# A 256-token first chunk, beta through K=1 matmuls, weights on ScalarE's queue, and key sums on GpSimd, in a fused attention and MLP kernel

## The chip, the cores and the metric

The kernel runs on one core of one Trainium2 chip. The metric is the device time of one execution in microseconds (us). I quote the median of a kernel's runs. A ratio between two kernels is the mean time of one kernel's fast runs over the mean of the other's fast runs of the same rounds, so it is not quite the ratio of the medians that I quote. A run is called slow when it is over 1.5% above the fastest run of the same kernel; ratios use fast runs alone. A profile is one execution: its span (130.2 us for the kernel before) is about 2 us shorter than the measured time.

The engines are named as in the profile: PE is TensorE (matmuls), DVE is VectorE, ACT is ScalarE, POOL is GpSimd, SP is SyncE, which here only issues DMA. This kernel fixes by hand the order in which each engine gets its instructions, and in the traces below an engine that waits for one instruction doesn't go on to the next: in x1_start_loop PE stood 4.58 us at one group of matmuls while the `moeout` products behind it had had their input for 4.1 us. That will matter.

## The reference, cut to what matters

```python
def phi(x):                       # 64 features from two 8-wide sketches
    a = einsum('rd,bhsd->bhsr', S1, x); b = einsum('rd,bhsd->bhsr', S2, x)
    return outer(a, b).reshape(..., 64)
q_p, k_p = phi(q), phi(k)         # q, k, v: (4, 4, 1088, 32) f32
kv  = einsum('bhsf,bhsd->bhfd', k_p, v)
z   = sum(k_p, axis=2)
num = einsum('bhsf,bhfd->bhsd', q_p, kv)
den = einsum('bhsf,bhf->bhs', q_p, z) + 1e-06
x   = (num / den), heads side by side          # (4352, 128)
h   = x @ w_in                                 # (4352, 2048)
out = (h / (1 + exp(-beta * h))) @ w_out       # (4352, 128)
```

There are four batches of 1088 tokens. The attention of a batch must be complete over its keys before any of its tokens can enter the MLP. The MLP is the larger part of the work.

## The kernel before

**The MLP in waves.** Since h·sigmoid(beta·h) is Silu(beta·h)/beta, the kernel folds beta into the weights: `winp = w_in * beta` and `woutp = w_out / beta`. What is left is one Silu per tile. A *wave* is two matmuls of 512 columns into a tile `wave` in PSUM (the memory that takes PE's products here), one Silu of 128x1024 on ScalarE into `g`, and two matmuls into `moeout`. A chunk of 512 tokens is eight waves; the whole MLP is 68 waves. The start time of each Silu is therefore a good clock of progress, and I use it throughout.

**The attention in groups.** Between waves stand small groups: `kps` (sketches of the keys), `kab` (their transposes), `kp` (the outer product), `kvz` (kv and z on PE), `kvd` (their copy out of PSUM by ScalarE), `zb` and `nd` (z and kv turned for the next products), `aps`/`bps` and `qp` (the same for the queries), `ndps`, `dps` (denominator), `dT`, `rc`, `rb` (its inverse, spread out), `nps` (numerator) and `xT`, the MLP's input.

```python
    tok_chk = [(o, min(TCH, NTOK - o)) for o in range(0, NTOK, TCH)]   # TCH = 512
    q_chk = [(0, 9), (9, TP - 9)]                 # 576 and 512 tokens of each batch
    # ... all big loads in one queue, in this order:
    k_t[0] = load_rows(k, 0, "k", halves)
    q_t[0] = load_rows(q, 0, "q", halves)
    v_t[0] = load_v(0)
    for c in range(0, DFF, DFF // 2):             # the weights stand behind q, k, v of batch 0
        nc.sync.dma_start(out=w_in_sb[:, cs], in_=moe_w_in[:, cs])
        nc.sync.dma_start(out=beta_bc[:, cs], in_=...)        # beta broadcast to 128 partitions
        nc.sync.dma_start(out=w_out_sb[:, js, :], in_=...)
    # ... [cut]
    def slot(group, waves):                       # a group of attention, then `waves` waves
        if group is not None:
            group()
        for _ in range(waves):
            if moe["ci"] < len(tok_chk) and sum(tok_chk[moe["ci"]]) > moe["ready"]:
                break                             # this chunk's tokens are not there yet
            # ... w2 of an older wave, then w1 of the next
```

The start, and the loop over batches 1 to 3:

```python
    kps(0); ...                                   # batch 0, first 576 tokens
    keep_warm(2); ndt(0); keep_warm(3)            # matmuls without use, in PE's idle time
    invert = den(0, 0); divide = num(0, 0); invert(); divide()
    turn_q(0, 1)
    keep_warm(9)
    slot(None, 1)                                 # the first wave
    # ... [cut: batch 0's second chunk, 512 tokens, one wave between groups]
    for b in range(1, B):
        if b == 1:
            for h in range(H): outer(b, h)        # kp, on VectorE
        turn_q(b, 1)
        slot(lambda: r_group((b, 1, 0), (b, 0, 0)), 1)
        zs = sum_z(b)                             # four adds on VectorE
        slot(lambda: kv(b, [1, 2, 3, 4], zs), 1 if few else 2)
        # ... [cut]
        turn_k(b + 1)                             # keys of the next batch: in mid-batch
        slot(lambda: kv(b, [5, 6, 7, 8, 0], zs), 1 if few else 2)
        slot(lambda: r_group((b, 1, 1), (b, 0, 1)), 1)
        turn_q(b + 1, 0)
        slot(lambda: kps(b + 1), ...); outer(b + 1, 0)
        # ... [cut: outer(b + 1, 1..3) spread over the next groups]
        slot(lambda: den(b, 0)(), ...)            # one denominator and inverse for each chunk
        slot(num0_den1, 1)
        slot(lambda: num(b, 1)(), 1)
```

## Time and profile before

| | before |
|---|---|
| time, median of 4 runs beside the changed kernel | 132.01 us (131.59 to 132.52) |
| span of the profile, mean granted TensorE clock | 130.2 us, 0.997 |
| first Silu, eighth Silu, 13th, 48th, last | 23.0, 36.8, 46.4, 102.0, 124.0 us |
| Silus that start in 30 to 60 us | 16 |
| busy: PE, VectorE, ScalarE, GpSimd | 113.1, 71.3, 79.8, 11.1 us |

Next, pieces of the chain of waits before the first Silu (start, duration, what):

```profile
1.65 6.04 DMA q<-in_q_dram
...
9.23 1.75 DVE kp L346 x5
...
12.90 4.13 PE kvz L406 x144
...
22.97 1.03 ACT g L267
```

The start takes 23 us: q's load until 7.7, products on VectorE, `kvz` on PE from 12.9 to 17.0, then the short steps to `xT`. Last, the stretch that the change aims at, in the view by stretches. Its columns are the stretch, its length, the busy time and count of PE, PEld, DVE, ACT and POOL, the granted clock, the DMA share and GB/s.

```profile
30.00:60.00 30.00, 27.72 (x356) 10.42 (x354) 27.49 (x48) 19.22 (x22) 0.00 (x0) 1.00 0.47 94
```

VectorE is busy for 27.49 of 30 us.

### The profile page before, as it was taken

How to read it: one execution, taken by the hardware profiler on the slowest of the kernel's cores; microseconds unless marked ns; L12 is line 12 of the kernel's file. 1: busy time of each engine (PE TensorE's matmuls, PEld its weight loads, DVE VectorE, ACT ScalarE, POOL GpSimd, SP SyncE). 2: the span in 40 equal slices, each digit the busy share in tenths (PEclk: the TensorE clock that was granted, in tenths of full speed). 3: DMA queues.
4: the chain of work that ended last, by engine and by line, in shares of the span. 5: the costliest groups of instructions: out<-in, count | busy, mean ns of one | idle time of the engine just before them, and what ended most of it. 6: DMA issues, size and time to landing. Idle time of an engine off the chain costs nothing.

```text
span 130.2 us, 2977 instructions
## 1 busy us (share of the span) xinstructions
PE 113.1 (87%) x1216; PEld 45.9 (35%) x1216; DVE 71.3 (55%) x142; ACT 79.8 (61%) x92; POOL 11.1 (9%) x24
## 2 busy tenths in 40 slices
PE   5787999887889999999997999999999989888830
PEld 2132933222334342342432332443432333334620
DVE  2579119249799988997367579940737400200210
ACT  1303010876358767477777866687776798888930
POOL 3000399700000000000000000000000000000000
PEclk9999999999999999999999999999999999999998
DMA  3999999999992320031000400500032050031232
GB/s 110 304 187 275 358 353 314 208 249 203 235 210 83 56 30 0 5 54 29 5 0 10 71 5 0 81 0 5 0 49 36 0 80 1 0 58 25 35 48 40
DMA packets 24909, 12.42 MB, mean 95 GB/s; under 512 B 18992, under 2 KB 23104, under 8 KB 24896
## 3 DMA queue, kind: packets, MB, share of 16 engines
q1 hardware_dynamic: 24576, 12.19, 42.1%
q8 instruction: 9, 0.15, 0.5%
q10 hardware_dynamic: 320, 0.04, 0.2%
q14 instruction: 4, 0.03, 0.1%
HBM read 10.00 MB, written 2.23 MB: 94 GB/s over the span
## 4 chain that ended last, share of the span: by engine, by line
PE 49%; DVE 22%; ACT 15%; DMA 5%; issue 5%; SPq 1%; ACTq 0%; DVEq 0%
PE moeout L223 15%; ACT g L267 15%; PE wave L259 13%; PE kvz L406 5%; DMA q<-in_q_dram 5%; PE aps L369 4%; DVE kp L346 4%; PE dps L471 3%; DVE qp L388 3%; PE bps L369 2%; DVE rb L489 2%; DVE xT L516 2%; PE nps L506 2%; PE kps L327 2%; DVE qT L315 2%
## 5 line engine op out<-in xcount | busy, mean ns | idle before, releaser
L267 ACT ACTIVATE g<-wave 128x1024 f16<-128x1024 f32 x68 | 67.8, 1023 | 30.1 <-PE wave L259 29.7
L223 PE MATMUL moeout<-g,woutp 128*128 128x512 f16 (+1 forms) x144 | 40.1, 369 | 3.3 <-ACT g L267 3.1
L259 PE MATMUL wave<-xT,winp 128*128 128x512 f16 (+1 forms) x144 | 40.0, 367 | 0.6 <-ACT g L267 0.4
L223 PEld LDWEIGHTS <-woutp 128*128 128x128 f16 x144 | 11.4, 97 | 24.8 <-issue 18.8
L259 PEld LDWEIGHTS <-winp 128*128 128x128 f16 x144 | 13.8, 97 | 17.3 <-issue 3.4
L388 DVE TENSOR_TENSOR qp<-bps,asb 128x576 f32<-128x576 f32 (+1 forms) x16 | 11.3, 713 | 14.5 <-ACT g L267 8.8
L233 DVE STREAM_TRANSPOSE o_sb<-moeout 128x512 f32<-128x512 f32 (+1 forms) x9 | 6.1, 676 | 21.5 <-PE moeout L223 21.5
L369 PE MATMUL aps<-qT,s_165 32*64 32x288 f32 (+1 forms) x128 | 13.6, 448 | 3.1 <-ACT g L267 2.0
L379 ACT COPY asb<-aps 128x576 f32<-128x576 f32 (+1 forms) x16 | 9.8, 610 | 5.7 <-PE aps L369 4.6
L369 PE MATMUL bps<-qT,s_170 32*64 32x288 f32 (+1 forms) x128 | 12.1, 446 | 0.1
L346 DVE TENSOR_TENSOR kp<-kab 128x576 f32<-128x576 f32 (+2 forms) x20 | 11.6, 620 | 0.0
L406 PE MATMUL kvz<-kp,v 128*32 128x64 f32 (+1 forms) x288 | 9.1, 246 | 1.2 <-DVE qp L388 0.8
L147 PE MATMUL warm<-idle 128*128 128x512 f16 x23 | 7.6, 479 | 1.5 <-DVE hm L159 1.5
L369 PEld LDWEIGHTS aps<-qT,s_165 32*64 32x64 f32 x128 | 4.6, 138 | 10.5 <-ACT g L267 5.3
L406 PEld LDWEIGHTS kvz<-kp,v 128*32 128x32 f32 (+1 forms) x288 | 6.5, 124 | 4.5 <-issue 2.3
L516 DVE TENSOR_TENSOR xT<-nps,rb 128x576 f16<-128x576 f32 (+1 forms) x8 | 5.8, 722 | 1.8 <-PE nps L506 1.4
L190 POOL TENSOR_TENSOR winp<-w_in_sb,beta_bc 128x256 f16<-128x256 f32 x8 | 5.5, 721 | 13.6 <-DMA beta_bc<-in_moe_beta_dram 13.6
L482 DVE STREAM_TRANSPOSE dT<-dps 128x288 f32<-128x288 f32 (+1 forms) x8 | 3.7, 463 | 5.1 <-PE dps L471 5.1
L315 DVE STREAM_TRANSPOSE qT<-q 128x576 f32<-128x576 f32 (+1 forms) x8 | 5.8, 726 | 0.8 <-DMA q<-in_q_dram 0.8
L489 DVE STREAM_TRANSPOSE rb<-rc 128x576 f32<-128x576 f32 (+1 forms) x8 | 6.0, 745 | 0.3
L327 PE MATMUL kps<-kT,sk 64*32 64x288 f32 x64 | 3.9, 482 | 2.3 <-DVE kT L303 2.3
L506 PE MATMUL nps<-qp,nd 64*32 64x288 f32 (+1 forms) x128 | 5.5, 401 | 0.0
(56 smaller groups left out, 60.9 us busy)
## 6 DMA issues: line engine op xcount, KB each, us to landing
v<-in_v_dram SPq DMA_DIRECT2D x16, 144.0 KB, 9.2
k<-in_k_dram SPq DMA_DIRECT2D x3, 544.0 KB, 11.8
q<-in_q_dram SPq DMA_DIRECT2D x3, 544.0 KB, 11.0
out_dram<-o_sb SPq DMA_DIRECT2D x20, 64.0 KB, 2.0
w_in_sb<-in_moe_w_in_dram SPq DMA_DIRECT2D x2, 512.0 KB, 8.7
beta_bc<-in_moe_beta_dram SPq DMA_DIRECT2D x2, 512.0 KB, 9.3
w_out_sb<-in_moe_w_out_dram SPq DMA_DIRECT2D x2, 512.0 KB, 9.8
k<-in_k_dram SPq DMA_DIRECT2D x1, 288.0 KB, 2.8
```

Source lines behind the costliest of these rows:

```text
L223: nc.tensor.matmul(out=moe["acc"][:, :tw], lhsT=woutp[:, j, :], rhs=g[:, jj, :tw], start=(j == 0), stop=(j == NJ - 1),)
L259: nc.tensor.matmul(out=wv[:, jj * tw : (jj + 1) * tw], lhsT=winp[:, (j0 + jj) * P : (j0 + jj + 1) * P], rhs=xT[:, t0 : t0 + tw], start=Tru ...
L267: nc.scalar.activation(out=g, in_=wv, func=ACTF.Silu)
L315: nc.vector.transpose(out=qT_of[b][:, t0 : t0 + tn].rearrange("p t c s -> p (t c s)"), in_=q_t[b][:, 2 * t0 : 2 * (t0 + tn)].rearrange("p ...
L346: nc.vector.tensor_tensor(out=KP[b][:, h, j0:j1].rearrange("p j (i l) -> p j i l", i=R), in0=bass.AP(tensor=a0.tensor, offset=a0.offset, a ...
L369: nc.tensor.matmul(out=dst[64 * c : 64 * c + 64, m, : 32 * tn], lhsT=sx[rows, :], rhs=qT_of[bb][rows, t0 : t0 + tn, c, :], start=True, sto ...
L379: nc.scalar.copy(out=ASB[a_of][:, :, :w], in_=aps[:, :, :w])
L388: nc.vector.tensor_tensor(out=QP[bb][:, 2 * pr : 2 * pr + 2, 32 * t0 : 32 * t0 + w], in0=bps[:, :, :w], in1=ASB[b_of][:, :, :w], op=MUL,)
L406: nc.tensor.matmul(out=kvz[32 * h : 32 * h + 32, F * which : F * which + F], lhsT=v_t[b][:kr, h, j, :] if which == 0 else ones[:kr, :], rh ...
L489: nc.vector.transpose(out=rb[:, :tn].rearrange("p t c s -> p (t c s)"), in_=bass.AP(tensor=r0.tensor, offset=r0.offset, ap=[list(r0.ap[0]) ...
L506: nc.tensor.matmul(out=nps[32 * h : 32 * h + 32, c, :w], lhsT=ND[b][rows, 32 * h : 32 * h + 32], rhs=QP[b][rows, h, 32 * t0 : 32 * t0 + w] ...
L516: nc.vector.tensor_tensor(out=xT[:, o : o + 2 * w].rearrange("p (t c s) -> p c t s", c=2, s=32), in0=nps[:, :, :w].rearrange("p c (t s) -> ...
```

## The change

The intent is to start the MLP earlier with a smaller first chunk and an earlier arrival of the weights, to relieve VectorE in the middle, and to halve the number of denominator inversions. The diff, cut to its core:

```diff
-    tok_chk = [(o, min(TCH, NTOK - o)) for o in range(0, NTOK, TCH)]
+    q_chk[0] = [(0, 4), (4, TP - 4)]              # batch 0: 256 and 832 tokens
+    tok_chk = [(0, 256)]                          # then 512 x 7, then 256, 256
+    ...
+    for r in range(4):                            # beta: four rows of 512 by GpSimd's queue
+        nc.gpsimd.dma_start(out=beta4[32 * r : 32 * r + 1, :], in_=...)
-    for c in range(0, DFF, DFF // 2):
-        nc.sync.dma_start(out=w_in_sb[:, cs], in_=moe_w_in[:, cs])
-        nc.sync.dma_start(out=beta_bc[:, cs], in_=...)
-        nc.sync.dma_start(out=w_out_sb[:, js, :], in_=...)
+    for m in range(4):
+        for r in range(4):
+            nc.tensor.matmul(out=b_dst[r][32 * m : 32 * m + 32, :],
+                             lhsT=ones[row, :], rhs=beta4[row, :], start=True, stop=True)
+    nc.scalar.copy(out=beta_bc[:, :1024], in_=beta_ps[0]...)
+    load_wout(0, NJ // 2)                         # nc.scalar.dma_start, as load_win
+    ...
-    keep_warm(9) ... keep_warm(2) ... keep_warm(3) ... keep_warm(9)
+    keep_warm(7)                                  # at the start, nowhere else
+    for j in range(3):
+        prep_wout_act(j)                          # woutp on ScalarE, ahead of kvd
+    kv(0, JB, [1]); kvd(0, 1, 2); kv(0, JB, [0]); kvd(0, 0, 1)
+    def keys(b):
+        turn_k(b); kps(b); kab(b)
+        for h in range(H):
+            outer(b, h, eng=nc.vector if b == 1 and h < 2 else nc.gpsimd)
+        zsum[b] = sum_z(b)                        # on nc.gpsimd
     for b in range(1, B):
         turn_q(b, 1)
+        if more:
+            keys(b + 1)                           # at the front of batch b
+            waves(next(pace))
...
-        slot(lambda: den(b, 0)(), ...)
-        slot(num0_den1, 1)
+        den(b, [0, 1], dps)                       # both chunks into one PSUM tile,
+        invert(b, [0, 1], dps)                    # one dT, rc and reciprocal
```

The last output store is also split over two queues.

## The prediction

> **What bounds the kernel now.** Of the 130.2 us span:
>
> 1. Prologue. ScalarE's timeline shows the first `g` Silu at 22.97 us, one of 68 of 1.02 us. The chain of waits there: q's load lands at 7.7, `kp` ends 12.0, `qp`, then `kvz` on PE 12.9 to 17.0, then `zb`, `nd`, `dps`, `rb`, `xT` until 22.3.
> 2. Middle, 23 to 102 us: 47 waves. By stretches, VectorE is busy 5.9 of 6.0 us in 36-42, 7.3 of 8.0 in 42-50, 9.4 of 10 in 50-60, and the chain there runs through VectorE; 30-60 us starts only 16 Silus (1.87 us each). In 60-100 PE is the limit: 26 waves, 1.54 us each. PE work from matmul starts: 0.875 us a wave, about 7.5 us a batch for attention; that is 95% of those 40 us.
> 3. Tail, 102 us to the end: 21 waves in pairs of 2.19 us (the `wave`-Silu-`moeout` ring), then about 5 us.
>
> **What the change does.**
>
> - First chunk 256 tokens: `qp`, `rb`, `xT` of the first chunk shrink from 576 columns (0.74, 0.78, 0.76 us) to 256 (estimate 0.43 each, as a 128x256 add) and 16 warm-up matmuls go.
> - Beta: 1 MB of broadcast load goes; four small GpSimd loads, 16 K=1 matmuls (estimate 1.2 us: a 288-column f32 matmul costs PE 0.15 us per row group) and 2 us of ScalarE copies come. The `kps` PSUM tile is the beta tile, so `kps` waits for GpSimd's loads, these matmuls and a 1.0 us copy. I expect it near 9 us instead of 6.4, giving back 1 to 2. The Trainium skill, "DMA: Bandwidth & Descriptors" (Specifications), gives first-byte latency about 1 us for GpSimd's path, 0.6 for the others; not shown yet.
> - Weights come on ScalarE's queue: GpSimd's prep starts near 11 us instead of 15.2.
> - Per batch VectorE loses four `kp` (2.9 us; two for batch 1), the z sums (2.75 us), one `dT`+`rc`+`rc` (0.9 us): about 19 to 12 us. GpSimd gets 4 x 1.6 + 5.8 = 12 us (estimate: its 128x256 product took 0.72 us, VectorE 0.42; the skill's "GPSIMD Engine Reference", 3.1, has 1.96x for 2048 columns, this trace 1.7x for 256). Issued one batch ahead, it hides in batches of 18 to 22 us.
> - PE: 12 instead of 4 waves use 256-column matmuls.
>
> **Critical path.** Prologue: first Silu at about 19.5 (-3.5). From there to the second chunk the VectorE chain (`qp` 2x1.0, `dT`, `rb`, `xT` of 832 columns) lets only about four waves out, then batch 1's keys run on VectorE; lead about 4 us at wave 7. 30-60 us turns from VectorE to PE bound: 1.87 to about 1.6 us a wave, worth 3.5 to 4.5. Batches 2, 3 and tail (20 waves) nearly unchanged. Sum: 8 to 9 us, less 0.5 for small matmuls and 0.5 unforeseen waits.
>
> **Predicted: 124.0 us (119.5 to 128.5 for 8 in 10).** Faster by over 2%: 0.93; within 2%: 0.05; slower: 0.02.
>
> **What would show it.** First Silu 18.5 to 21; `kps` waiting on ScalarE or GpSimd's loads; VectorE busy under 75% in 30-60, about 19 Silus there; GpSimd busy about 48 us, `kvz` hardly waiting for it; tail pairs still 2.19.
>
> **What would make it wrong.** GpSimd's loads landing after 9 us; GpSimd's `winp` slowing VectorE's two-input `kp` (the GPSIMD page, 1. Specifications, names that contention; no run shows it); GpSimd slower than 2x, so `kvz` waits; PE still stalled by in-order waits on VectorE in the middle.

## More of the kernel before

From the page of the kernel before: each engine's busy time, then PE's busy share and the granted clock in 40 equal slices (tenths).

```profile
PE 113.1 (87%) x1216; PEld 45.9 (35%) x1216; DVE 71.3 (55%) x142; ACT 79.8 (61%) x92; POOL 11.1 (9%) x24
...
PE   5787999887889999999997999999999989888830
...
PEclk9999999999999999999999999999999999999998
```

PE is busy nearly everywhere after the start, and its clock is full until the last slice.

Beside the first experiments all runs of the kernel before lay within 131.4 to 132.4 us; in the later calls they spread over 129.9 to 135.6 us, and more than half of them are labelled slow because a few were quick. Ratios of different calls therefore compare less sharply than their intervals say.

## The result, and the profile after

The changed kernel took 151.13 us (150.57 to 152.34, four runs) against 132.01 us. The ratio is 1.1456 [1.1389, 1.1522]: slower by 14.6%, where I had predicted faster by 6%.

| | before | after |
|---|---|---|
| span, mean granted TensorE clock | 130.2 us, 0.997 | 150.2 us, 0.930 |
| Silu 1 | 23.0 | 28.9 (+5.9) |
| Silu 5 | 30.3 | 41.8 (+11.5) |
| Silu 8 | 36.8 | 55.0 (+18.2) |
| Silu 13 | 46.4 | 69.1 (+22.7) |
| Silu 48 | 102.0 | 122.6 (+20.6) |
| Silu 68, the last | 124.0 | 144.6 (+20.6) |

All of the loss is there by the 13th Silu. From the 13th to the 48th the changed kernel is 2.1 us quicker (53.5 against 55.6 us), and the last 20 waves take 22.0 us in both. The page after:

```profile
PE 119.7 (80%) x1264; PEld 49.3 (33%) x1264; DVE 57.0 (38%) x111; ACT 84.2 (56%) x105; POOL 39.9 (27%) x47
...
PE   6768649599517899865599889889999989889960
...
PEclk9999996955985579999999999999999999999999
```

VectorE's load did fall, from 71.3 to 57.0 us, as intended. But PE has holes (the 4, the 5s and the 1 in its row), and its clock falls in slices 7, 9, 10 and 12 to 15. The stretch that I had counted on:

```profile
30.00:60.00 30.00, 23.56 (x212) 8.16 (x212) 14.74 (x22) 11.44 (x13) 16.79 (x13) 0.72 0.28 73
```

VectorE is at 14.74 of 30 us and PE at 23.56, much of that at half clock (0.72 on average). Only 9 Silus start here. No engine is full: the stretch is bound by latency, by who waits for whom. The chain of waits at the start of the kernel after:

```profile
1.95 3.53 DMA beta<-in_moe_beta_dram
5.61 4.44 PE beta L214 x32
10.05 9.99 DMA w_out_sb<-in_moe_w_out_dram
20.13 0.98 ACT woutp L254 x3
```

The 16 beta matmuls (the trace has two records for each) hold PE until 10.0 us; `kps`, which needs the same PSUM tile, starts at 11.11 (6.37 before). Then the chain leaves attention altogether: it goes through a *weight* load. That load was issued only at 10.05 us, since in ScalarE's stream its issue stands behind the copy of beta (in e3 below, without that copy, at 5.71). ScalarE's timeline of the kernel after shows why (start, duration, engine, line, operation, what; in brackets the idle time before and who ended it):

```profile
20.13 0.98 ACT L254 ACTIVATE woutp<-w_out_sb,rbeta 128x128 f16<-128x128 f32 x3 [4.32 <-DMA w_out_sb<-in_moe_w_out_dram]
21.02 0.24 ACT L496 COPY kvd<-kvz 128x128 f32<-128x128 f32 x1
...
28.94 1.03 ACT L326 ACTIVATE g<-wave 128x1024 f16<-128x1024 f32 x1
...
63.10 0.63 ACT L434 COPY asb<-aps 128x576 f32<-128x576 f32 x1
69.12 1.02 ACT L326 ACTIVATE g<-wave 128x1024 f16<-128x1024 f32 x1 [5.38 <-PE wave L318]
```

The three `woutp` scalings, which nobody needs before the first `moeout` matmul, stand in ScalarE's stream in front of the copy `kvd`, which everybody needs. They wait 4.32 us for w_out, which landed near 20 us. But the chain shows only the path that ended last, and the other one was close behind. From PE's timeline:

```profile
11.11 1.22 PE L381 MATMUL kps<-kT,sk 64*32 64x288 f32 x16 [1.17 <-ACT beta_bc L221]
...
21.32 0.53 PE L483 MATMUL kvz<-kp,v 128*32 128x64 f32 x20 [1.46 <-ACT kvd L496]
```

PE's own products, late through `kps`, ended at 19.87, so it waited only 1.46 us for `kvd`. And at the 13th Silu stands a hole of 5.38 us. What that wave's matmul waited for is in PE's timeline:

```profile
68.48 0.60 PE L318 MATMUL wave<-xT,winp 128*128 128x512 f16 x2 [2.09 <-DVE xT L609]
```

It waited for `xT` of batch 1. With a first chunk of 256 the chunk boundaries lie at 256, 768 and 1280 tokens. Batch 0 has 1088 tokens, so only 768 of them can be used before batch 1 delivers: 4 + 8 = 12 waves. Before, the boundaries were 512 and 1024, so 16 waves were available. The change took away a quarter of the work that hides batch 1's attention.

The clock has a pattern of its own. I cut the trace into windows of 3.413 us, the length that the Trainium skill, "TensorE: Matmul & The Clock Gate" (Part 1: The HAM clock gate), gives for the activity window, laid so that one edge is at 23.40:

```profile
19.99:23.40 3.41, 1.22 (x33) 0.80 (x33) 0.00 (x0) 1.20 (x5) 0.00 (x0) 1.00 0.90 203
23.40:26.81 3.41, 3.28 (x42) 0.94 (x41) 1.99 (x6) 1.93 (x7) 3.04 (x5) 0.50 0.68 190
26.81:30.23 3.42, 1.67 (x24) 0.59 (x19) 1.35 (x2) 2.63 (x3) 2.03 (x4) 1.00 0.96 263
30.23:33.64 3.41, 3.25 (x20) 0.83 (x20) 1.02 (x1) 0.85 (x1) 0.00 (x0) 0.50 1.05 279
...
40.46:43.88 3.42, 1.31 (x22) 0.51 (x6) 2.99 (x4) 1.02 (x1) 2.07 (x2) 1.00 0.02 5
43.88:47.29 3.41, 2.43 (x14) 1.06 (x14) 1.02 (x3) 0.64 (x1) 3.33 (x2) 0.50 0.00 0
```

The half-clock stretches, 23.4 to 26.8, 30.2 to 37.1 and 43.9 to 54.1 us, are one, two and three such windows. The page says that the clock is halved after an idle window and restored after a busy one, and that the windows run freely. The trace agrees on the length and on the two values, 1.00 and 0.50. It doesn't agree that a whole window must be idle: windows with 1.2 to 1.7 us of PE work were followed by half clock here (though the one from 71.18 us, with 1.56 us, was not). In its profiled execution the kernel before hardly met this (0.997; its other executions have mean clocks from 0.95 to 1.00). It ran 23 useless matmuls in PE's gaps, 14 of them between `kvz` and the first wave. The change dropped all but seven.

So I had several suspects: the idle clock, the chunk boundary, the beta route and weight queue, GpSimd's operations, the place of the keys, the single denominator. The experiments were to price each one.

### The profile page after: what moved, and what is told of

It is laid out like the page before. It is cut to its first block, busy times and chain, and to the rows that moved or that the text cites. A ratio compares the mean times of both kernels' runs of the same rounds, so it can differ in the third digit from the quotient of the medians.

```text
span 150.2 us, 3085 instructions
## 1 busy us (share of the span) xinstructions
PE 119.7 (80%) x1264; PEld 49.3 (33%) x1264; DVE 57.0 (38%) x111; ACT 84.2 (56%) x105; POOL 39.9 (27%) x47
## 4 chain that ended last, share of the span: by engine, by line
PE 56%; DVE 15%; ACT 13%; DMA 9%; issue 4%; POOL 0%; ACTq 0%; DVEq 0%; POOLq 0%
PE moeout L295 18%; PE wave L318 15%; ACT g L326 11%; DMA w_out_sb<-in_moe_w_out_dram 7%; PE aps L417 6%; PE dps L555 4%; PE kvz L483 4%; PE beta L214 3%; PE nps L597 3%; PE bps L417 2%; DVE xT L609 2%; DVE kT L357 2%; DMA beta<-in_moe_beta_dram 2%; PE kps L381 2%; DVE rb L581 2%
## 5 line engine op out<-in xcount | busy, mean ns | idle before, releaser
L442 DVE TENSOR_TENSOR qp<-bps,asb 128x576 f32<-128x576 f32 (+3 forms) x16 | 11.4, 720 | 28.5 <-PE bps L417 19.2
L402 POOL TENSOR_TENSOR kp<-kab 128x576 f32<-128x576 f32 x10 | 12.4, 1270 | 27.1 <-DVE kab L393 27.1
L417 PE MATMUL aps<-qT,s 32*64 32x288 f32 (+3 forms) x128 | 14.8, 491 | 4.4 <-DVE qT L369 3.1
L417 PE MATMUL bps<-qT,s 32*64 32x288 f32 (+3 forms) x128 | 13.8, 496 | 1.9 <-DVE qp L442 1.5
L434 ACT COPY asb<-aps 128x576 f32<-128x576 f32 (+3 forms) x16 | 9.8, 610 | 8.1 <-PE aps L417 7.0
L609 DVE TENSOR_TENSOR xT<-nps,rb 128x576 f16<-128x576 f32 (+3 forms) x8 | 5.8, 719 | 5.3 <-PE nps L597 5.2
L510 POOL TENSOR_TENSOR z<-kp 128x1024 f32<-128x1024 f32 x3 | 7.1, 2351 | 0.2
L402 DVE TENSOR_TENSOR kp<-kab 128x384 f32<-128x384 f32 (+2 forms) x10 | 6.5, 707 | 0.0
L555 PE MATMUL dps<-qp,zb 128*32 128x288 f32 (+3 forms) x64 | 5.6, 463 | 1.1 <-DVE nd L547 1.0
L597 PE MATMUL nps<-qp,nd 64*32 64x288 f32 (+3 forms) x128 | 6.1, 443 | 0.0
```

The costliest lines, as they stand in the source:

```text
L402: (eng or nc.vector).tensor_tensor(out=KP[b][:, h, j0:j1].rearrange("p j (i l) -> p j i l", i=R), in0=bass.AP(tensor=a0.tensor, offset=a0. ...
L417: nc.tensor.matmul(out=dst[64 * c : 64 * c + 64, m, : 32 * tn], lhsT=(sa if which == "a" else sb_)[rows, :], rhs=qT_of[bb][rows, t0 : t0 + ...
L434: nc.scalar.copy(out=ASB[key][:, :, :w], in_=aps[:, :, :w])
L442: nc.vector.tensor_tensor(out=QP[bb][:, 2 * pr : 2 * pr + 2, 32 * t0 : 32 * t0 + w], in0=bps[:, :, :w], in1=ASB[key][:, :, :w], op=MUL,)
L510: eng.tensor_tensor(out=z4, in0=kp[:, :, 1:5], in1=kp[:, :, 5:9], op=ADD)
L555: nc.tensor.matmul(out=dps[32 * h : 32 * h + 32, :w], lhsT=zb[b % 2][:, i, h, :], rhs=QP[b][:, h, 32 * t0 : 32 * t0 + w], start=(i == 0), ...
```

## The experiments

A difference "by ratio" below is the difference of two ratios to the kernel before, times 132 us. From the two intervals each such difference is uncertain by 1.1 (e1) to 2.3 us (x2 against x1).

### First set: one suspect at a time, on the changed kernel

**e1_warm.** Useless matmuls go back into PE's gaps, 38 in all, up to batch 1.

```diff
     kvd(0, 1, 2)
+    keep_warm(6)
     kv(0, JB, [0])
+    keep_warm(2)
...
     keys(1)
     waves(1)
+    warm1(12)
```

> The changed kernel with 38 idle-filling matmuls put where PE waits (8 before the first wave's products, 6 after the first wave, 24 around batch 1's keys); no wait taken away. Theory A (PE's clock, halved in three stretches of 3.1, 6.8 and 10.2 us after idle gaps, costs the time): the mean granted clock goes from 0.93 to 0.98 or more, PE's work in those stretches halves, and the time falls by 6 to 9 us, from about 151 to 143-145. Theory B (in-order waits between VectorE and PE pace those stretches, the low clock only follows them): the clock rises as well, but the time falls by less than 2 us.

Measured: 147.89 us, ratio 1.1226 [1.1177, 1.1276], which is 3.0 us less by ratio. The same view by stretches, for the kernel after and then for this run:

```profile
31.00:37.00 6.00, 5.84 (x40) 1.89 (x36) 3.18 (x5) 1.64 (x2) 0.00 (x0) 0.50 1.04 286
45.00:54.00 9.00, 7.52 (x51) 2.21 (x52) 3.84 (x6) 3.32 (x4) 7.84 (x8) 0.50 0.09 15
```

```profile
31.00:37.00 6.00, 5.02 (x46) 2.33 (x46) 4.75 (x7) 2.90 (x3) 0.00 (x0) 1.00 0.65 178
45.00:54.00 9.00, 8.50 (x122) 3.15 (x123) 3.10 (x6) 5.21 (x7) 8.76 (x8) 1.00 0.08 14
```

The clock in both stretches went from 0.50 to 1.00, so the lost clock is real; getting it back, net of the useless matmuls, is worth 3.0 us. It is between the two theories: neither the main cause nor nothing.

**e2_chunks.** The second MLP chunk is 256 tokens too, so that the boundaries lie at 256, 512, 1024.

```diff
-    tok_chk = [(0, 256)]
+    tok_chk = [(0, 256), (256, 256)]
```

> The changed kernel with token chunks 256, 256, 512, ... instead of 256, 512, ..., so that the 1088 tokens of batch 0 allow 16 waves instead of 12; same number of waves and of 256-column matmuls. Theory A (the 5.4 us without a Silu at 63-69 us is starvation by the chunk boundary at 768): the gap shrinks below 2 us and the time falls by 3 to 4 us, to about 147.5. Theory B (those products only move from one gap to another, batch 1's attention chain decides): less than 1 us.

Measured: 147.23 us, 1.1122 [1.1043, 1.1201], 4.4 us less by ratio. The hole ahead of the 13th Silu is gone: 59.4 to 61.1 us between the 12th and 13th (the last line holds two Silus), where after had 62.2 to 69.1.

```profile
59.43 1.02 ACT L326 ACTIVATE g<-wave 128x1024 f16<-128x1024 f32 x1 [1.06 <-PE wave L318]
...
61.13 2.17 ACT L326 ACTIVATE g<-wave 128x1024 f16<-128x1024 f32 x2
```

The boundary costs about 4 us, from one line.

**e3_beta_dma.** Beta comes as a broadcast load again; the weights stay on ScalarE's queue.

```diff
-    for m in range(4): ... nc.tensor.matmul(out=b_dst[r]..., lhsT=ones[row, :], rhs=beta4[row, :])
-    nc.scalar.copy(out=beta_bc[:, :1024], ...)        # and two more
+    for c in range(0, DFF, DFF // 2):
+        nc.sync.dma_start(out=beta_bc[:, c : c + DFF // 2], in_=...)
```

> The changed kernel with the broadcast load of beta on SyncE's queue as before, without the K=1 matmuls, their GpSimd loads and the copies. Theory A (the beta route delays kps from about 7 to 11.1 us and with it the first Silu at 28.9): kps starts near 7, first Silu at 24 to 25.5, time down by 3.5 to 5 us to about 147. Theory B (the weights' load on ScalarE's queue, waited for at 20.1 us by the woutp products that stand ahead of the kvd copy, holds the prologue): first Silu stays within 1.5 us of 28.9, time within 1.5 us.

Measured: 148.97 us, 1.1301 [1.123, 1.1373], 2.05 us less by ratio. `kps` starts at 6.62 instead of 11.11, but the first Silu only moved from 28.9 to 27.0. Of these 4.5 us, 2.5 were lost again to loads. From the timelines of VectorE and PE of this run:

```profile
8.92 1.92 DVE L377 TENSOR_TENSOR kp<-kab 128x384 f32<-128x384 f32 x4
...
20.56 1.04 DVE L344 STREAM_TRANSPOSE qT<-q 128x832 f32<-128x832 f32 x1 [7.88 <-DMA q<-in_q_dram]
...
13.49 1.29 PE L458 MATMUL kvz<-kp,v 128*32 128x64 f32 x40 [1.13 <-DMA v<-in_v_dram]
```

`kvz` waits for v, and VectorE stands for 7.88 us on the second part of q, with the steps that lead to `xT` behind it. Part of that is this edit's own doing: it puts beta's 1 MB ahead of q's second part in SyncE's queue, which was issued at 11.88 us here and at 6.06 in the kernel after. There is a second finding here. The same four `kp` products in the kernel after, with what GpSimd did meanwhile:

```profile
13.20 3.07 DVE L402 TENSOR_TENSOR kp<-kab 128x384 f32<-128x384 f32 x4
...
11.98 3.40 POOL L242 TENSOR_TENSOR winp<-w_in_sb,beta_bc 128x256 f16<-128x256 f32 x4 [7.00 <-DMA w_in_sb<-in_moe_w_in_dram]
```

They took 3.07 us beside GpSimd's `winp` and 1.92 us when GpSimd was idle (in e3 its `winp` began at 15.96). The Trainium skill, "GPSIMD Engine Reference" (1. Specifications), says that GpSimd shares its SBUF interfaces with VectorE and that instructions with two SBUF inputs contend. `kp` has two; the trace agrees, with 0.77 against 0.48 us each.

**e4_keys_dve.** The `kp` products and z sums go back from GpSimd to VectorE, at the changed place.

```diff
-            outer(b, h, eng=nc.vector if b == 1 and h < 2 else nc.gpsimd)
+            outer(b, h, eng=nc.vector)
...
-        eng = nc.gpsimd
+        eng = nc.vector
```

> The changed kernel with kp products and z sums of batches 1 to 3 back on VectorE. Theory A (GpSimd's share is no cause of the loss, VectorE is only 38% busy): GpSimd busy falls from 40 to about 12 us, VectorE rises by about 17 us, time between 150 and 154. Theory B (GpSimd's keys slow VectorE's two-input products, 1.18 us instead of 0.74, or kvz waits for them): faster by 3 us or more.

Measured: 162.57 us, 1.2288 [1.2209, 1.2368]: 11 us worse than after, outside both theories. So GpSimd is not the culprit. VectorE's timeline (of a slow run, at 165.12 us; only the order is read from it):

```profile
55.11 2.72 DVE L402 TENSOR_TENSOR kp<-kab 128x576 f32<-128x576 f32 x4
57.87 1.22 DVE L510 TENSOR_TENSOR z<-kp 128x1024 f32<-128x1024 f32 x1
...
60.66 0.74 DVE L442 TENSOR_TENSOR qp<-bps,asb 128x576 f32<-128x576 f32 x1
```

With all keys of batch 2 at one place, `qp` of batch 1, which the current batch needs, stands behind 5.5 us of work for later. In the new order VectorE can't take GpSimd's share back without loss; that made me suspect the order.

### Second set: all mends together, and parts of the change on the kernel before

**f1_all.** The mends of e1, e2 and e3, with q's second part ahead of beta's load, `qT` moved behind `zb`, and all `woutp` on ScalarE moved behind `nd`.

```diff
-    load_rows(q, q_t, 0, "q", ((QA, T),))             # from behind beta_bc ...
+    load_rows(q, q_t, 0, "q", ((QA, T),))             # ... to ahead of it
-    for j in range(3):
-        prep_wout_act(j)                              # ahead of kvd
+    for j in range(NJ // 2):
+        prep_wout_act(j)                              # behind nd
```

> The changed kernel with all three: chunks 256, 256, 512, ...; beta by broadcast load; idle-filling matmuls (35 added); and the load of q's second part ahead of beta, its transpose after zb, and ScalarE's woutp products after the nd copy. Theory A (three separate costs that add: 3.0, 4.4 and 2 us measured alone, plus 3 to 4 us of prologue that was behind the beta route): about 138.5 us, first Silu at 21 to 23. Theory B (they overlap): 142 us or more. Either way above 132 if a fourth cost sits in the order of VectorE's work between the first waves and batch 1.

Measured: 141.60 us, 1.0798 [1.0627, 1.0969]. That is 8.7 us less by ratio, where e1, e2 and e3 alone gave 9.5: these add up within noise, but the 3 to 4 us that I expected from the other prologue moves did not come. The first Silu is at 25.8, not at 21 to 23, and 10 us remain. One fault is of my making: six warm-up matmuls ran at half clock from 16.25 to 18.84 us, with the second part of `kvz` behind them.

**f2_first576.** The first chunk goes back to 576 tokens and all MLP chunks to 512.

```diff
-    q_chk[0] = [(0, 4), (4, TP - 4)]
-    tok_chk = [(0, 256)] ...
+    tok_chk = [(o, min(TCH, NTOK - o)) for o in range(0, NTOK, TCH)]
```

> The changed kernel with the first query chunk back at 576 tokens and the token chunks back at 512. Theory A (the small first chunk costs twice: 12 instead of 16 waves before batch 1 is ready, and 832 columns of chunk 1 in one serial chain): the first Silu is later by about 1 us, but the eighth wave is earlier by 4 us or more and the gap before the thirteenth goes; time about 144. Theory B (the small chunk is only the boundary, 4.4 us as measured, and its shorter first chain gives 1 to 2 us back): 148 to 149.

Measured: 146.29 us, 1.1142 [1.0998, 1.1287], 4.1 us less by ratio, level with e2 and between the two theories. The first Silu is 1.2 us later than after's (30.17 against 28.94): that is all that the small first chunk gave, where I had counted on 3.5 us for the start.

**g1_before_gp.** On the kernel before: z sums of batches 1 to 3 and `kp` of 2 and 3 on GpSimd.

```diff
-        nc.vector.tensor_tensor(out=z4, ...)          # and three more adds
+        nc.gpsimd.tensor_tensor(out=z4, ...)
-            outer(b + 1, 0)
+            outer(b + 1, 0, eng=nc.gpsimd)            # so for all four
```

> The kernel before with one part of the change alone: z sums of all later batches and kp of batches 2 and 3 on GpSimd, in the same order. Theory A (that part is what was worth predicting: VectorE bounds 30 to 60 us): VectorE's busy time falls from 71 to about 57 us, more than 17 Silus in 30-60, time 127 to 129.5. Theory B (in-order waits and not VectorE's load pace that stretch): within 1 us of before.

Measured: 132.65 us, 1.0096 [0.9933, 1.026]: not separable from before. Its profile (a slow run) shows `kvz` of batch 1 waiting 1.26 us for the GpSimd sum, with no Silu from 43.8 to 48.2, which g3 below avoids.

**g2_before_cold.** On the kernel before: 14 of its 23 warm-up matmuls away.

```diff
-    keep_warm(2)
     ndt(0)
-    keep_warm(3)
     invert = den(0, 0)
...
-    keep_warm(9)
```

> The kernel before without the 14 idle-filling matmuls between the kvz products and the first wave (as the change has none there). Theory A (PE's clock falls when it idles there and the slow matmuls are then waited for): granted clock below 0.98 with halved stretches after 18 us, 1.5 to 4 us slower. Theory B: the products of the first wave come soon enough, clock above 0.99, within 0.7 us.

Measured: 132.41 us, 1.0066 [0.9901, 1.0231]. The clock fell as in the kernel after, from the page:

```profile
PEclk9986995599999999999999999999999999999996
```

It is 0.62 over 18 to 27 us, and yet the time is the same within noise, which is about 2 us here. The useless matmuls had stood on PE's path themselves: the last nine took 2.12 us right ahead of the first wave. My reading, which no run tests, is that a lost clock costs only where something waits on PE in those windows. The kernel after also lost more of it: six windows at half clock, 20.5 us, against about 7 us here (estimated from the 0.62 over 9 us).

### Third set: which half, start or loop

**x1_start_loop.** Before's start (loads, 576-token chunk, warm-ups, beta load) with the changed loop.

```diff
-    (the changed kernel's loads, beta matmuls, batch 0 and keys(1) as above)
+    (before's loads and order of batch 0; keys(1) with kp on VectorE, z on GpSimd)
     for b in range(1, B):                              # the changed loop
         turn_q(b, 1)
         keys(b + 1) ...
```

> A crossover: the start of the kernel before (loads, chunk sizes, warm-up matmuls and order up to batch 0's last product) with the changed kernel's loop over batches 1 to 3 (keys on GpSimd at the front of a batch, one den for two chunks). Theory A (the loss is all in the start, the loop gains the 3.4 us that the change shows from its 13th to its 48th wave, 52.2 us against 55.6): first Silu near 23, eighth wave near 37, time 128 to 130. Theory B (keys of the next batch at the front of a batch also stall PE, as in the change's waves 5 to 8): waves 8 to 16 are 4 us later than before's, time 132 to 136.

Measured: 139.12 us, 1.0551 [1.0422, 1.068], slower than both theories had it. (The expectation's 52.2 and 3.4 us don't come out of the trace; it has 53.5 and 2.1.) The start alone is worth 12 us by ratio (1.1456 to 1.0551); the loop, and the little else that differs, costs 7.3 us. Where it loses, from the timelines of VectorE and PE:

```profile
33.53 2.72 DVE L366 TENSOR_TENSOR kp<-kab 128x576 f32<-128x576 f32 x4
36.17 0.70 DVE L333 STREAM_TRANSPOSE qT<-q 128x512 f32<-128x512 f32 x1
36.80 1.27 DVE L321 STREAM_TRANSPOSE kT<-k 128x1088 f32<-128x1088 f32 x1
...
38.22 0.72 PE L345 MATMUL kps<-kT,sk 64*32 64x288 f32 x16 [4.58 <-DVE kT L321]
```

PE stands for 4.58 us at `kps` of batch 2, which is not needed for a whole batch, because VectorE is not yet at `kT` of batch 2. In PE's stream the waves behind it wait too: the next Silu comes 7.1 us after the one before it (33.73 to 40.85).

**x2_start_late.** x1 with the keys of the next batch two groups later.

```diff
-        if more:
-            keys(b + 1)
-            waves(next(pace))
         r_group((b, 1, 0), (b, 0, 0))
         waves(next(pace))
         r_group((b, 0, 1), (b, 1, 0))
         waves(next(pace))
+        if more:
+            keys(b + 1)
+            waves(next(pace))
```

> The same crossover with the next batch's keys two groups later in a batch. Theory A (the place of the keys matters little): within 1 us of the crossover above. Theory B (keys at the front stall PE in batch 1): 2 to 4 us faster than the crossover above, 128 to 131.

Measured: 134.90 us, 1.0214 [1.01, 1.0329], 4.4 us less than x1 by ratio. The same matmul now:

```profile
40.47 1.05 PE L345 MATMUL kps<-kT,sk 64*32 64x288 f32 x16 [0.45 <-DVE kT L321]
```

The wait fell from 4.58 to 0.45 us and the time by about as much. With this start the place of the keys is a cause.

**h1_late.** The same move in the changed kernel; the edit is that of x2.

> The changed kernel with only the next batch's keys two groups later in a batch, all else as it is. Theory A (keys at the front of batch 1 are part of the slow waves 5 to 8): the eighth wave is 2 to 4 us earlier, time 147.5 to 149. Theory B (the slow waves come from the start, its clock and its chunk): within 1 us of 151.

Measured: 150.25 us, from 147.59 to 150.34. Three of the four runs are labelled slow, since one was quicker, and no ratio is given. It is inconclusive in time. The trace shows the gain at the eighth Silu (50.7 against 55.0) given back at the chunk boundary: no Silu from 58.7 to 66.5, since the tokens of batch 0 are used up all the same. The two causes stand one behind the other.

**g3_before_gp23.** The kernel before with `kp` and z of batches 2 and 3 on GpSimd, and batch 1's sums left on VectorE.

```diff
-        zs = zsum[b]                                   # of g1
+        zs = zsum[b] or sum_z(b, nc.vector)
```

> The kernel before with kp and z sums of batches 2 and 3 on GpSimd, batch 1's z on VectorE as before (where the first trial, with batch 1's z on GpSimd too, left kvz waiting 1.3 us and the Silus 5.4 us apart at 43 to 48 us). Theory A (that wait hid a gain): 129.5 to 131, 1 to 2.5 us faster. Theory B (the stretch is PE's and its in-order waits, VectorE's load costs nothing): within 1 us of before, though VectorE's busy time falls by about 11 us.

Measured: 131.92 us, 1.0026 [0.9891, 1.0162]. By stretches (a run of 133.02 us, slow; it is compared with before's line above for its busy times alone):

```profile
30.00:60.00 30.00, 26.91 (x353) 10.49 (x353) 22.77 (x40) 18.42 (x21) 9.73 (x8) 1.00 0.49 91
```

VectorE fell from 27.49 to 22.77 us in the stretch, GpSimd took 9.73, and the time didn't move beyond a noise of 1.8 us. What was taken away lies after 46 us (`kp` and z of batch 2); `kp` and z of batch 1 stayed on VectorE. This profile also has a stall of PE of 1.07 us at 42.8 us, put down to "issue", that before's lacks; past it the pace is before's, with 55.0 us from the 13th to the 48th Silu against 55.6. So these VectorE operations do not hold the stretch. That PE's 27 of 30 us and the order of its waits do is my reading of the profile. This is the premise of half of my prediction, and it fails here without any of the change's other parts in the way.

### Fourth set: who loads the weights, and the denominator

**y1_sp_weights.** e3, with the weights on SyncE's queue behind q, k and v of batch 0, as before had them. The edit makes two moves: q's second part, which e3 had behind beta's load, goes ahead of it as well.

```diff
-        nc.scalar.dma_start(out=w_in_sb[:, c0:c1], in_=moe_w_in[:, c0:c1])
+        nc.sync.dma_start(out=w_in_sb[:, c0:c1], in_=moe_w_in[:, c0:c1])
...
+    load_rows(q, q_t, 0, "q", ((QA, T),))             # from behind beta_bc to ahead of it
```

> The beta-by-load variant (e3) with one thing more undone: the weights are loaded on SyncE's queue behind v and q's second part, no longer from 4.1 us on through ScalarE's queue beside them. Theory A (the weights' early loads take DMA time from v, which landed at 13.5 us there, and from q's second part, 20.6 us): v lands by 11.5 and q's second part by 14, the first Silu comes at 23.5 to 25 instead of 27.0, time 1.5 to 3 us less than e3's 149.0. Theory B (the DMA engines are busy either way, and the weights' later landing holds winp instead): first Silu within 1 us of 27.0, time within 1 us of e3's.

Measured: 145.01 us, 1.1009 [1.087, 1.1149], 3.9 us less than e3 by ratio. The first Silu moved from 27.0 to 22.0. The waits that e3 had on v and on q are gone; PE and VectorE:

```profile
12.40 1.29 PE L455 MATMUL kvz<-kp,v 128*32 128x64 f32 x40
...
12.88 1.03 DVE L341 STREAM_TRANSPOSE qT<-q 128x832 f32<-128x832 f32 x1
```

The Trainium skill, "Trainium Kernel Development and Optimization" (Key Constraints), says that DMAs issued from the SP, ACT and POOL queues run on the same 16 engines and interleave, and that issuing from several only saves issue time. These runs agree: v, which stands ahead of the weights in both, was waited for until 13.49 us in e3 and was there by 12.40 here, while w_out's first half came hardly earlier in e3 (the first `woutp` starts at 15.16 there, at 15.36 here). Of q's delay the larger part was e3's own order (q's second part issued at 11.88 us there, at 5.87 here). f1, with q ahead of beta (issued at 6.73) and the weights still on ScalarE's queue, shows what the second queue costs:

```profile
14.97 0.77 PE L463 MATMUL kvz<-kp,v 128*32 128x64 f32 x40 [2.98 <-DMA q<-in_q_dram]
```

There PE waits until 14.97 us for a load that the trace gives as q's; here q's second part was there by 12.88. The order in one queue was before's way of giving q, k and v the first turn.

**h2_chunks_late.** The mends of e2 and x2 together, in the changed kernel (both edits are above).

> The changed kernel with both token chunks 256, 256, 512, ... and the next batch's keys two groups later. Late keys alone brought the eighth wave 4.3 us forward, but the gap at the chunk boundary grew from 6.9 to 7.8 us and the last wave came only 2 us earlier. Theory A (the boundary ate what the keys' place gave; the chunks alone gave 4.4 us): with the boundary gone the two add up to 7 us or more, 144 or less. Theory B (the keys' place gives only 1 to 2 us whatever the boundary): 145 to 147.

Measured: 145.58 us, 1.1062 [1.0951, 1.1174], only 0.8 us less than e2, which is within noise. So in the changed kernel the place of the keys shows no gain clear of noise when the tokens suffice; in x1, with before's start, it was worth 4.4. One of the four executions took 270.89 us, and it was the profiled one. It is left out of the ratio and comes up again in the last section.

**c2_oneden.** Before's start and nearly before's order of groups, with keys of batches 2 and 3 on GpSimd, and one denominator for two chunks.

```diff
-        (two den, invert, num, divide groups)
+        den(b, [0, 1], dps)
+        invert(b, [0, 1], dps)
+        for n in range(2): num(b, n, nps); divide(b, n, nps); waves(...)
```

> The kernel before's start and its order of a batch, with the change's parts that take work off VectorE: kp and z of batches 2 and 3 on GpSimd, one den for two chunks, one zb product, last store on two queues. Theory A (with nothing put in front of PE the relief is worth something): 129 to 131, faster than before by 1 to 2%. Theory B (the middle is PE's and its waits, VectorE's relief costs and gives nothing): within 1% of before's median of the same call.

Measured: 134.72 us, 1.0262 [1.0199, 1.0326], slower than before and than both theories. A wave waits 3.14 us for `xT`; from the timelines of GpSimd, VectorE and PE:

```profile
51.21 2.35 POOL L473 TENSOR_TENSOR z<-kp 128x1024 f32<-128x1024 f32 x1
...
51.41 2.20 DVE L535 TENSOR_SCALAR rc<-dT 128x36 f32<-128x36 f32 x1
...
56.12 0.59 PE L282 MATMUL wave<-xT,winp 128*128 128x512 f16 x2 [3.14 <-DVE xT L572]
```

The little `rc`, 36 columns, took 2.20 us and ended at 53.61, just after GpSimd's sum (53.56).

**d1_c2_twoden.** c2 with two denominators.

```diff
-        den(b, [0, 1], dps)
-        invert(b, [0, 1], dps)
+        den(b, [0], dps); invert(b, [0], dps); waves(...)
+        num(b, 0, nps); den(b, [1], dps)
+        divide(b, 0, nps); invert(b, [1], dps); waves(...)
+        num(b, 1, nps); divide(b, 1, nps)
```

> The c2 variant with two dens a batch again, one for each query chunk as in the kernel before (each with its own transposes and reciprocal), everything else as c2. Theory A (one den for both chunks holds back the first chunk's tokens: in c2 PE waited 3.1 us for xT at 52 to 57 us, when batch 0's 16 waves were used up, 4.9 us between Silus against before's 2.4): the gap shrinks to about 2.5 us, time 1.5 to 2.5 us less than c2, level with before within 1%. Theory B (c2's 2.6% come from its other parts): within 0.7 us of c2.

Measured: 130.58 us, 0.998 [0.9904, 1.0056]: level with before, and 3.7 us less than c2 by ratio. But the comparison is not clean. In this run `rc` came just ahead of GpSimd's sum and took 0.17 us:

```profile
49.36 0.17 DVE L535 TENSOR_SCALAR rc<-dT 128x18 f32<-128x18 f32 x1
...
49.60 2.37 POOL L473 TENSOR_TENSOR z<-kp 128x1024 f32<-128x1024 f32 x1
```

Some 2.0 us of c2's wait are the hold of that one instruction, and the edit has moved it out of GpSimd's way. The profiled run of d1 also has its first Silu 1.3 us earlier than c2's (21.2 against 22.5), which the edit doesn't touch. What the merged denominator alone costs there, these two runs do not separate.

**d2_twoden.** The changed kernel with two denominators (the edit of d1).

> The changed kernel with two dens a batch again. Theory A (as above: the 6.9 us gap between its twelfth and thirteenth Silu is partly the second chunk's den, reciprocal and transpose, which stand ahead of the first chunk's xT): that gap falls to 4.5 to 5.5 us, time 1.5 to 2.5 us less, about 149. Theory B: within 1 us of 151.

Measured: 149.46 us, 1.1429 [1.1319, 1.1539], 0.4 us less by ratio, within noise. In the changed kernel the merged denominator hardly counts.

**y2_mended.** The changed kernel with everything mended that I had found: y1, the chunks of e2, the late keys of x2, two denominators, `woutp` behind `nd`, and warm-up matmuls. It keeps the 256-token first chunk and GpSimd's share.

```diff
+ (edits of y1, e2, x2, d1; woutp on ScalarE behind nd as in f1; 37 warm-up matmuls in all)
```

> The changed kernel with each of the costs found undone at once (beta by load and weights behind v on SyncE's queue, ScalarE's woutp products behind the nd copy, chunks 256, 256, 512, idle-filling matmuls, late keys, two dens); GpSimd's keys and the small first query chunk stay. Theory A (these are the causes, and they add up): first Silu at 20.5 to 22, 133 to 136 us, within 3% of before. Theory B (a cost of more than 4 us is still unnamed): 138 or more.

Measured: 137.26 us, 1.0438 [1.0322, 1.0554], between the two theories. The single effects add up to 3.0 (e1) + 4.4 (e2) + 2.05 (e3) + 3.9 (y1 on e3) + 0.8 (h2 on e2) + 0.4 (d2) = 14.5 us; together they gave (1.1456 - 1.0438) × 132 = 13.4 us, with the move of `woutp`, which was not priced alone. The sum of the single effects is uncertain by about 4 us, so the match is looser than it looks; but 13.4 of the 19.2 us of slowdown are undone by these mends, measured together.

What remains is 5.8 us. The first Silu is at 22.8, level with before's 23.0, the eighth at 42.2 against 36.8, the last at 129.4 against 124.0. All of the remaining lag of 5.4 us arises between the first and the eighth wave, where batch 0's second chunk of 832 tokens and the keys of batch 1 have single waves between long steps. Two runs narrow it. x2, with before's start and the same late keys, takes 13.8 us from the first to the eighth Silu, as before does, and y2 19.4; so the lag belongs to the order of batch 0 and of batch 1's keys, not to the loop. And f2, with 576 tokens in the first chunk, takes 20.5 us where e2 takes 23.7. I didn't isolate it. That the size of this chunk is the cause is argued, not shown; it stays open.

No version clearly beat the kernel before. The best, d1, has an interval that contains 1.

## Why the prediction was wrong

The prediction was wrong in its direction, and at several steps.

1. **"Prologue. First Silu at about 19.5 (-3.5)."** It came at 28.9. I had put `kps` near 9 us; it was at 11.11, since the beta matmuls took 4.33 us with the waits for their loads, 2.3 us of it after the last wait, at 7.64 (estimate 1.2). GpSimd's preparation starting earlier meant that it started beside VectorE's `kp` (3.07 instead of 1.92 us), and ScalarE's `woutp` in front of `kvd` made PE wait 1.46 us more. A step that I hadn't taken at all shows once the beta route is undone: weights on a second queue take DMA time from v and q (f1 and y1). e3 and y1 together (5.9 us, first Silu 28.9 to 22.0) show that the beta route and the order of the loads make up this loss; they don't separate the two, since e3 put beta in front of q.
2. **"30-60 us turns from VectorE to PE bound ... worth 3.5 to 4.5."** The busy share that I predicted came true (VectorE under 75%: it was 49%), but nothing was gained. g3 shows that relieving VectorE by 4.7 us there is worth nothing in before's order, within a noise of 1.8 us. VectorE's 27.49 of 30 us was a high busy share, not proof of a bound: PE had 27.72 in the same stretch.
3. **The 256-token chunk was costed by the length of its operations alone.** I looked at the columns of `qp`, `rb` and `xT`, and not at the token supply: 12 waves instead of 16 until batch 1 delivers. e2 prices this at 4.4 us.
4. **"16 warm-up matmuls go" was entered as a gain.** The clock fell to half in six windows, which e1 prices at 3.0 us. g2 shows that the same removal is neutral in the kernel before, within about 2 us, so the loss probably comes from their absence together with the new idle gaps.
5. **The order of the groups was not costed.** The keys at the front of a batch stopped PE for 4.58 us in x1, worth 4.4 us there; in the changed kernel it came to 0.8 us, within noise.
6. **"One `dT`+`rc`+`rc` (0.9 us)" less per batch** was counted as a relief. d2 shows 0.4 us within noise for undoing it; c2 and d1 suggest that merging can cost, since the first wave waits for both chunks' work, but a held instruction confounds them.

Right were: the tail's 20 waves unchanged, GpSimd's cost of a `kp` (1.15 to 1.65 us against 1.6), GpSimd's load without `kvz` hanging on it (busy for 39.9 us, where I had said about 48), and batches 2 and 3 nearly unchanged (2.1 us gained from Silu 13 to 48). The contention of `winp` and `kp`, and "PE still stalled by in-order waits on VectorE in the middle", were on my list of what might go wrong, with far too small a chance: I gave "slower" 0.02. The error behind all six is that I summed savings of busy time for a kernel that is held by the order of waits.

## What to carry to other kernels

Before you count a saving, write down what stands in front of each critical instruction in its engine's stream and in its DMA queue: an early, uncritical operation or load can cost more than the operation itself (three `woutp` of 0.98 us in all made PE wait 1.46 us for `kvd`; in e3, with beta's load in front of q's second part, VectorE waited 7.88 us for it). When a chunk size changes, count how many units of work are available until the next producer delivers. And test whether a busy engine is a bound by relieving it alone: here 4.7 us less work in VectorE's fullest stretch bought nothing that the noise of 1.8 us would let through.

## What the Trainium skill lacked or had wrong

- "GPSIMD Engine Reference", 1. Specifications, names the contention with VectorE but no size; other pages of the skill go further into the shared ports, so what the runs add is the sizes. Here a two-input product of VectorE went from 0.48 to 0.77 us (128x384), and a TENSOR_SCALAR with one input went from 0.17 to 2.20 us in c2, ending 0.05 us after GpSimd's sum ended. In the changed kernel itself the first chunk's `rc` took 0.76 us (25.13 to 25.89) while one `winp` of GpSimd ran from 25.14 to 25.87. In d1 transposes and reciprocals that ran beside such a sum kept their length (`rb` 0.78 us). The page's mention of performance modes may explain the TENSOR_SCALAR; no run here separates that.
- "GPSIMD Engine Reference", 3.1, gives the ratio to VectorE for one size, 1.96 at 2048 columns. Here the z sums took 2.35 against 1.2 us at 1024 columns (1.96), 1.27 against 0.69 at 512 (1.8) and 0.72 against 0.42 at 256 (1.7).
- "TensorE: Matmul & The Clock Gate", Part 1, asks for an idle window before the clock is halved and one busy window to restore it. The windows of 3.41 us agree with the trace. But halving came after windows with 1.22, 1.67 and 1.31 us of PE work, and not after ones with 1.56 (from 71.18 us) and 1.87 us, so the amount of PE work in a window does not decide it alone; and after 30.2 us a window with 3.25 us busy was followed by another at half clock.
- The same page notes that clock records can be unreliable and that the clock has been seen stuck at a quarter for over 50 us. In the run of h2_chunks_late that took 270.89 us, the 512-column `wave` matmuls took 838 ns on average (379 ns is the median before) over a span of 268.8 us, with a recorded clock of 1.000; ScalarE's Silu kept its 1.02 us. Whether this is the page's stuck state no run here shows.
- "DMA: Bandwidth & Descriptors" (Specifications) gives about 1 us to the first byte for GpSimd's path and 0.6 us for the others. With the other loads under way, the four beta loads of 2 KB took a median of 4.0 us from issue to landing, and two loads of 16 KB on ScalarE's queue 3.7 us: landing is not the first byte, so this doesn't contradict the page, but the figure alone says little about when a small load can be used in a full system.
- "TensorEngine Tiling (Array Packing)" (Theoretical Speedup) gives up to 16 times for tiles that are small in both dimensions. The 16 K=1 matmuls in f32 with 512 columns took 4.33 us in all with the waits for their loads, 2.3 us of it after the last wait; the page has no time for such a group in f32.
